# Linear attention with gated experts: a written order of all units found anew, and the place where a flag is read

## The chip, the cores and the metric

The kernel runs on one core of a Trainium2 chip. The time is device time in microseconds (us). It is the median of 3 runs. PE is TensorE, DVE is VectorE, ACT is ScalarE, POOL is GpSimd, and SP is the engine that issues most transfers here.

## The reference

Two stages follow each other. The first is linear attention, the second sends each token through one of eight experts:

```python
q_p, k_p = (phi(q), phi(k))          # phi(x) = (x if x > 0 else exp(x) - 1) + 1
kv = np.einsum('bhsd,bhse->bhde', k_p, v)
z = np.sum(k_p, axis=2)
num = np.einsum('bhsd,bhde->bhse', q_p, kv)
den = np.einsum('bhsd,bhd->bhs', q_p, z)[..., None] + 1e-06
x = num / den                        # (8, 8, 576, 64) -> x: (8, 576, 512)
...
logits = x @ w_gate                  # 8 experts
local_gate = sigmoid(x @ w_local)
for b in range(B):
    for s in range(S):
        fresh_e = argmax(logits[b, s])
        e = fresh_e if s == 0 or local_gate[b, s] < 0.5 else prev_e
        h = np.maximum(x[b, s] @ w1[e], 0.0)
        out[b, s] = softmax(logits[b, s])[e] * (h @ w2[e])
```

Batch 8, heads 8, sequence 576, head dimension 64; w1 is 8 x 512 x 1024, w2 is 8 x 1024 x 512.

## The kernel before

The kernel takes for granted that all tokens of a batch use the expert of its first token, and counts the tokens for which that would be wrong. Only if the count (the flag) is over zero does it run a general path behind the main one, which these inputs don't reach.

The main path is cut into units, each of which is one function. A string, ORDER, names all units in the order in which they are written into the program. Each engine takes its own instructions strictly in that order, and semaphores hold it back where data or a buffer is not ready. A number behind a slash names one of four PSUM slots of two banks; the next unit in a slot waits until the last one there has been read out. A batch is a (0 to 7), and half a batch's heads is n = 2a + j (0 to 15). The units:

- Lk.n, Lv.n, Lq.n: SP issues the load of k, v or q (576 KB). There are 4 buffers for k, 3 for v and 2 for q, so Lk.6 waits until K.2 has read its buffer, Lq.7 until P.q.5 is done. Lwg loads the gate's weights. SP also issues the stores ST and, in HOLD, a tiny copy that waits for the first expert's weights.
- E.x.n, E2.x.n: exp and relu on ACT (x is k or q); P.x.n: DVE combines them to phi; CL.n, P0.0 and E0.0 are forms of this for the first batch. VC.n copies v beside a column of ones (DVE; VC.0 on ACT).
- K.n: PE's 36 small matmuls of k with v (tile kvps, 64x64 tiles, line 297), KC.n copies the result out (DVE).
- Q.n, QL.a: transposes of q on PE (tq, tql), QC.n and QLC.a copy them out (ACT).
- N.a.j.h, NL.a: q with kv (nps, npl, 64x64 tiles, line 349 and 368); D and DL divide on DVE.
- X.a.h, XL.a: transposes of the quotient (tx, txl); XC, XLC copy them to xT (DVE).
- R.a.0, R.a.1: the gate's logits (lps; R.a.0 has 64 columns of the array); RC copies them out; PK.a picks the expert, BK.a books it in a small table of which weights are on the core; W.a.0 and W.a.1 have POOL load w1 and w2 if they are missing; CW.a.x copies them to the place of use (DVE). S1, S2, S3 work out the probability.
- H.a.m: the hidden layer in 8 pieces of 8 matmuls (hps, line 532), HC.a.m applies the relu (ACT). O0.a and O.a.0 to O.a.4: the output layer (yps, lines 551 and 555; O.a.4 uses 128x64); OC.a.i scales and evicts (ACT).
- FL, TOT, FI count the flag (DVE, PE, DVE); FR.e has engine e read it into a register, ahead of its branch at the end.

The first matmuls, on a tile of zeros (fill, line 705), only keep PE busy until data comes.

Of the kernel before, what the change touches and what calls it, by code (L numbers as in the profile page):

```python
# [24 lines left out]
P.k.1 K.0/2 Lwg E2.q.0 VC.1 P.q.0.0 K.1/3 Lv.3 P.q.0 E.q.1 KC.0 KC.1 Lk.2 E2.q.1 NL.0/1 Q.0/2 Lq.2 DL.0
E.k.3 P.q.1.0 WG QC.0 XL.0/3 XLC.0 P.q.1 R.0.0/1 E2.k.3 N.0.0.1/3 RC.0.0 Lq.3 PK.0 Q.1/2 Lv.2 D.0.0.1 W.0.0
N.0.0.0/1 QC.1 VC.3 E.q.2 D.0.0.0 N.0.1.1/3 N.0.1.0/2 BK.0 D.0.1.1 E.k.2 W.0.1 D.0.1.0 E.q.3 X.0.1/1 P.k.3
E2.k.2 X.0.0/3 E2.q.3 XC.0.0 K.3/2 XC.0.1 E2.q.2 R.0.1/0 H.0.0/3 P.q.2 H.0.1/1 HC.0.0 RC.0.1 P.q.3 H.0.2/3
HC.0.1 H.0.3/0 HOLD P.k.2 HC.0.2 Lq.4 QL.1/1 H.0.4/3 Lq.5 QLC.1 KC.3 VC.2 HC.0.3 Lk.5 Q.3/2 Lk.4 CW.0.0
HC.0.4 Q.2/1 S1.0 H.0.5/0 QC.2 H.0.6/3 S2.0 HC.0.5 QC.3 K.2/1 HC.0.6 N.1.1.1/0 KC.2 Lv.6 N.1.0.1/2 D.1.1.1  # L30
E.q.4 NL.1/3 H.0.7/1 D.1.0.1 O0.0/0 HC.0.7 DL.1 E2.q.4 S3.0 O.0.0 XL.1/2 E.q.5 X.1.1/1 XLC.1 P.q.4 O.0.1/3
OC.0.0 E.k.5 XC.1.1 Lq.6 R.1.0/2 Lv.5 N.1.0.0/0 RC.1.0 OC.0.1 Lv.4 PK.1 N.1.1.0/1 E.k.4 O.0.2/2 D.1.1.0
W.1.0 E2.q.5 D.1.0.0 O.0.3/3 E2.k.5 P.q.5 OC.0.2 X.1.0/1 OC.0.3 O.0.4/0 XC.1.0 Lq.7 E.q.6 Lk.7 CW.1.0
R.1.1/2 QL.2/3 Q.4/1 QLC.2 RC.1.1 E2.k.4 CW.0.1 H.1.0/3 OC.0.4 VC.5 Q.5/2 W.1.1 HC.1.0 VC.4 QC.4 H.1.1/0
P.k.4 Lv.7 E.q.7 Lk.6 H.1.2/3 BK.1 H.1.3/1 HC.1.1 P.k.5 HC.1.2 K.4/0 E2.q.6 S1.1 K.5/3 HC.1.3 KC.4 CW.1.1
S2.1 QC.5 H.1.4/0 Lk.9 P.q.6 H.1.5/1 HC.1.4 KC.5 Lq.8 VC.6 N.2.0.1/2 HC.1.5 ST.0.0 NL.2/0 E.k.6 D.2.0.1
N.2.0.0/3 N.2.1.0/1 Lk.8 E.k.7 DL.2 Lv.8 H.1.6/2 ST.0.4 D.2.1.0 H.1.7/0 HC.1.6 S3.1 E2.k.7 XL.2/1 O0.1/2
D.2.0.0 HC.1.7 O.1.0 XLC.2 O.1.1/0 VC.7 OC.1.0 P.k.7 E2.k.6 R.2.0/3 E2.q.7 N.2.1.1/1 P.k.6 K.7/2 E.q.8
RC.2.0 P.q.7 O.1.2/3 E.k.9 KC.7 Lq.9 D.2.1.1 OC.1.1 X.2.0/2 E.k.8 K.6/0 XC.2.0 PK.2 OC.1.2 QL.3/1 Lk.10
X.2.1/2 QLC.3 Lv.9 Q.7/3 E2.k.8 KC.6 W.2.0 XC.2.1 Lk.11 Q.6/1 QC.7 P.k.8 NL.3/0 QC.6 O.1.3/2 DL.3 W.2.1  # L40
E2.q.8 VC.8 R.2.1/3 BK.2 E.q.9 XL.3/1 O.1.4/0 XLC.3 RC.2.1 CW.2.0 R.3.0/1 K.8/3 OC.1.4 E.k.10 VC.9 H.2.0/0
Lk.12 RC.3.0 KC.8 Lv.10 S1.2 H.2.1/1 HC.2.0 PK.3 OC.1.3 N.3.1.1/3 HC.2.1 P.q.8 N.3.1.0/0 W.3.0 E2.q.9
H.2.2/2 D.3.1.0 E2.k.9 Lq.10 H.2.3/1 D.3.1.1 HC.2.2 H.2.4/0 HC.2.3 P.k.9 H.2.5/2 HC.2.4 N.3.0.1/3 P.q.9
HC.2.5 K.9/1 E.q.10 D.3.0.1 Lq.11 N.3.0.0/0 E2.k.10 H.2.6/2 D.3.0.0 Q.9/3 HC.2.6 CW.2.1 S2.2 QL.4/0 Q.8/2
QLC.4 S3.2 W.3.1 QC.9 H.2.7/0 KC.9 VC.10 X.3.1/1 HC.2.7 P.k.10 O0.2/3 E2.q.10 XC.3.1 QC.8 X.3.0/0 P.q.10
O.2.0 NL.4/1 E.k.11 O.2.1/2 XC.3.0 Lq.12 OC.2.0 DL.4 E2.k.11 R.3.1/0 CW.3.0 XL.4/3 O.2.2/1 E.k.12 RC.3.1
XLC.4 E.q.11 O.2.3/0 OC.2.1 OC.2.2 N.4.1.1/3 OC.2.3 N.4.0.0/2 O.2.4/1 D.4.0.0 K.10/0 OC.2.4 D.4.1.1 E2.q.11
R.4.0/2 N.4.0.1/1 Lk.14 KC.10 Lv.11 H.3.0/3 P.q.11 Lv.12 ST.1.0 H.3.1/0 HC.3.0 D.4.0.1 H.3.2/3 ST.2.4 HC.3.1
RC.4.0 BK.3 H.3.3/1 Lv.13 HC.3.2 P.k.11 ST.1.4 QL.5/2 HC.3.3 H.3.4/0 CW.3.1 QLC.5 H.3.5/3 HC.3.4 Lk.13 S1.3
E.q.12 Q.11/1 VC.11 PK.4 HC.3.5 X.4.1/2 H.3.6/0 QC.11 Lq.13 W.4.0 K.11/3 HC.3.6 E2.q.12 N.4.1.0/1 KC.11  # L50
XC.4.1 N.5.1.1/0 E2.k.12 D.4.1.0 W.4.1 NL.5/3 H.3.7/2 S2.3 E.k.14 D.5.1.1 O0.3/1 HC.3.7 S3.3 X.4.0/0 DL.5
O.3.0 Q.10/2 P.k.12 OC.3.0 XL.5/3 O.3.1/1 XLC.5 E.k.13 XC.4.0 P.q.12 QC.10 R.4.1/3 O.3.2/0 CW.4.0 OC.3.1
Lq.14 Lv.14 E.q.13 O.3.3/2 VC.12 RC.4.1 N.5.0.1/1 OC.3.3 K.12/3 OC.3.2 D.5.0.1 O.3.4/2 KC.12 N.5.0.0/0
OC.3.4 R.5.0/1 E2.q.13 N.5.1.0/3 ST.3.4 RC.5.0 D.5.0.0 X.5.1/2 H.4.0/1 Lk.15 D.5.1.0 ST.2.0 H.4.1/0 HC.4.0
BK.4 E.q.14 Lv.15 H.4.2/3 PK.5 HC.4.1 H.4.3/1 P.q.13 HC.4.2 W.5.0 H.4.4/0 E2.k.13 XC.5.1 H.4.5/3 Lq.15
HC.4.3 S1.4 HC.4.4 QL.6/2 VC.13 Q.12/1 S2.4 HC.4.5 P.k.13 H.4.6/0 QLC.6 CW.4.1 H.4.7/3 HC.4.6 QC.12 X.5.0/2
W.5.1 K.13/0 HC.4.7 E2.k.14 N.6.0.0/1 KC.13 XC.5.0 N.6.0.1/3 E.k.15 NL.6/0 D.6.0.1 O0.4/2 E2.k.15 S3.4 O.4.0
E2.q.14 O.4.1/3 D.6.0.0 E.q.15 DL.6 O.4.2/1 E2.q.15 OC.4.0 P.q.15 Q.13/0 OC.4.1 O.4.3/2 QC.13 VC.15 CW.5.0
# [12 lines left out]
"""


# [1 line left out]
def kernel(  # L75
# [44 lines left out]
    with ExitStack() as main:  # L120
# [481 lines left out]
        def load_flag(engine):  # L602

            for r in flag_r:
                if r.engine == engine:
                    nc.reg_load(r, flag_i[0:1, 0:1])
# [345 lines left out]
```

## Time and profile before

| what | value |
|---|---|
| median of 3 runs | 223.32 us (222.03 to 223.62) |
| profiled execution | 224.62 us, of which span 222.4 us |
| PE, ACT, DVE, POOL busy | 206.8, 153.2, 151.6, 12.3 us |
| granted clock of PE | 0.996 |
| moved by DMA | 46.77 MB |

The span goes from the first to the last instruction of the program; 2.2 us of the profiled time lie around it. The profiled execution is one run, and 1.3 us above the median. PEld is PE's weight load, which overlaps its matmuls. A wait is put down to what ended it last; "issue" is time in which an engine waited for nothing that the profile shows.

### The profile page before, as it was taken

Reading aid. Unit: us, or ns where it says so; the run is one execution under the profiler, and the core shown is the slowest. Engines: PE = TensorE matmul, PEld = TensorE weight load, DVE = VectorE, ACT = ScalarE, POOL = GpSimd, SP = SyncE. Lnnn points to the kernel's source line nnn. Section 1 sums busy time; section 2 is a strip of 40 time slices with the busy share of each in tenths; the row PEclk is TensorE's granted clock in tenths of the full one; section 3 lists DMA queues with packets and bytes.
Section 4 is the critical chain, followed back from the end, with each engine's and each line's share of the span. In section 5 each row is a group of like instructions: output and inputs, shape, how many; then the busy total and the mean of one; then the engine's idle time right before and its main releaser. Section 6 shows DMA issues by size and latency. Waiting matters only on the chain.

```text
span 222.4 us, 8532 instructions
## 1 busy us (share of the span) xinstructions
PE 206.8 (93%) x3695; PEld 149.7 (67%) x3711; DVE 151.6 (68%) x428; ACT 153.2 (69%) x226; POOL 12.3 (6%) x41
## 2 busy tenths in 40 slices
...
GB/s 194 385 347 330 218 208 392 126 247 272 233 178 401 174 316 215 208 227 222 67 266 406 198 212 101 376 221 204 113 309 4 3 93 134 186 183 2 27 322 90
DMA packets 24141, 46.77 MB, mean 210 GB/s; under 512 B 2834, under 2 KB 8978, under 8 KB 23202
## 3 DMA queue, kind: packets, MB, share of 16 engines
...
q8 instruction: 31, 0.51, 0.9%
q10 hardware_dynamic: 432, 0.20, 0.4%
q14 instruction: 12, 0.10, 0.1%
...
## 4 chain that ended last, share of the span: by engine, by line
PE 84%; DMA 6%; DVE 3%; issue 2%; ACT 2%; SPq 0%; DVEq 0%; ACTq 0%
PE hps L532 27%; PE yps L551 25%; PE nps L349 8%; PE kvps L297 7%; PE tq L308 6%; PE tx L383 3%; PE yps L555 3%; DMA qraw<-in_q_dram 3%; DMA kraw<-in_k_dram 3%; PE lps L416 1%; DVE kraw L271 1%; PE npl L368 1%; PE lps L410 1%; PE fill L705 1%; PE tql L322 1%
## 5 line engine op out<-in xcount | busy, mean ns | idle before, releaser
L532 PE MATMUL hps<-xT,w1cur 128*128 128x288 bf16 x512 | 66.9, 286 | 0.8 <-issue 0.8
L551 PE MATMUL yps<-w2cur,hT 128*128 128x512 bf16 x241 | 58.4, 379 | 0.8
L532 PEld LDWEIGHTS <-w1cur 128*128 128x128 bf16 x512 | 48.7, 98 | 13.7 <-issue 1.3
L539 ACT ACTIVATE hT<-hps 128x576 bf16<-128x576 f32 x64 | 41.2, 652 | 24.3 <-PE hps L532 24.2
L551 PEld LDWEIGHTS <-hT 128*128 128x128 bf16 x256 | 24.1, 98 | 25.5 <-issue 0.2
L565 ACT ACTIVATE yo<-yps,pr 128x512 f32<-128x512 f32 x32 | 21.3, 686 | 12.9 <-PE yps L551 10.1
L276 DVE SCALAR_TENSOR_TENSOR fq<-fq,qraw 128x576 f32<-128x576 f32 (+1 forms) x32 | 22.5, 740 | 2.8 <-ACT qraw L247 2.8
L297 PE MATMUL kvps<-vone,kraw 64*64 64x65 f32 x1152 | 19.9, 220 | 3.2 <-ACT hT L539 1.2
L337 DVE TENSOR_TENSOR xb<-nps,rec 128x512 bf16<-128x512 f32 x32 | 22.1, 691 | 1.1
L349 PE MATMUL nps<-kv,qT 64*64 64x65 f32 x1024 | 21.1, 222 | 1.1 <-ACT qT L314 0.6
L297 PEld LDWEIGHTS kvps<-vone,kraw 64*64 64x64 f32 x1152 | 18.2, 134 | 5.4 <-ACT hT L539 1.5
L314 ACT COPY qT<-tq 128x512 f32<-128x512 f32 x32 | 18.3, 640 | 4.5 <-PE tq L308 4.5
L349 PEld LDWEIGHTS nps<-kv,qT 64*64 64x64 f32 x1024 | 17.6, 134 | 4.9 <-issue 2.7
L241 ACT ACTIVATE ek<-kraw 128x1152 f32<-128x1152 f32 x16 | 18.5, 1162 | 2.6 <-DMA kraw<-in_k_dram 2.2
L241 ACT ACTIVATE fq<-qraw 128x1152 f32<-128x1152 f32 (+1 forms) x16 | 18.5, 1156 | 2.4 <-DMA qraw<-in_q_dram 2.2
L269 DVE SCALAR_TENSOR_TENSOR kraw<-ek,kraw 128x1152 f32<-128x1152 f32 x14 | 18.8, 1346 | 0.3 <-ACT kraw L247 0.3
L247 ACT ACTIVATE qraw<-qraw 128x1152 f32<-128x1152 f32 (+1 forms) x16 | 18.3, 1150 | 0.1
L308 PE MATMUL tq<-ident,fq 128*128 128x128 f32 x128 | 16.4, 274 | 0.0
L247 ACT ACTIVATE kraw<-kraw 128x1152 f32<-128x1152 f32 x14 | 16.4, 1168 | 0.0
L308 PEld LDWEIGHTS tq<-ident,fq 128*128 128x128 f32 x128 | 14.3, 141 | 0.5
L388 DVE COPY xT<-tx 128x1024 bf16<-128x1024 bf16 x16 | 10.8, 681 | 3.5 <-PE tx L383 3.5
L302 DVE COPY kv<-kvps 128x130 f32<-128x130 f32 x16 | 4.6, 289 | 11.3 <-PE kvps L297 11.2
...
## 6 DMA issues: line engine op xcount, KB each, us to landing
...
```

The lines of the kernel that those rows point to most:

```text
L241: nc.scalar.activation(e[:, :, c0:c1, :], raw_, Act.Exp)
L247: nc.scalar.activation(raw_, raw_, Act.Relu)
L269: nc.vector.scalar_tensor_tensor(r, e, 1.0, r, Alu.min, Alu.add)
L276: nc.vector.scalar_tensor_tensor(e[:, g], e[:, g], 1.0, r[:, g], Alu.min, Alu.add)
L297: nc.tensor.matmul(ps[g * PH:(g + 1) * PH, t, :W], lhsT=f[h, g, c, :], rhs=vo[h, g, c, :], start=(c == 0), stop=(c == C - 1))
L308: nc.tensor.transpose(ps[:, r, i * P:(i + 1) * P], ex_[n, "q"][:, 1 + i + (NC - 1) * r, :, :], identity=ident)
L337: nc.vector.tensor_tensor(dst, ps[:, :, :, :Dh].rearrange("p g (i t) e -> p g i t e", t=2), rec.rearrange("p g (i t o) -> p g i t o", t=2, ...
L349: nc.tensor.matmul(ps[o * PH:(o + 1) * PH, g, (il * 2 + t) * W:(il * 2 + t + 1) * W], lhsT=qT[n][g * PH:(g + 1) * PH, t, i * P + o * PH:i ...
L532: nc.tensor.matmul(ps[:, u, :HS], lhsT=w1b[:, kk, m * P:(m + 1) * P], rhs=xT[b][:, kk, u * HS:(u + 1) * HS], start=(kk == 0), stop=(kk == ...
L539: nc.scalar.activation(hT[b][:, m, :].rearrange("p (u s) -> p u s", u=2), open_.pop(("H", b, m))[:, :, :HS], Act.Relu)
L551: nc.tensor.matmul(ps, lhsT=hT[b][:, m, i * P:(i + 1) * P], rhs=w2b[:, m, :], start=(m == 0), stop=(m == FK - 1))
L565: nc.scalar.activation(ym[:, i, :], ps, Act.Copy, scale=pr[:, i:i + 1])
```

## The change

The whole of ORDER is replaced: the same units stand in another order, and many have another PSUM slot. The lengths of units from which the order is found now count changes of the array's tiling. The number of instructions that compute is the same. The places at which the flag is read are given by ORDER alone, as before; a table beside it, which the program did not use, goes:

```diff
 ORDER = """
-Lk.1 FILL/0 Lk.0 Lv.0 Lq.0 Lv.1 E.k.1 Lq.1 E0.0 CL.0 E.k.0 CL.1 Lk.3 P0.0 VC.0 P.k.0 QL.0/1 QLC.0 E.q.0
...
+Lk.1 FILL/0 Lv.0 Lk.0 Lq.0 Lv.1 Lq.1 Lwg E.k.1 CL.1 Lk.3 E0.0 P.k.1 VC.0 P0.0 Lv.3 E.k.0 CL.0 QL.0/1 Lk.2
...
-        after = {"DVE": ("FI",), "POOL": ("FI",), "SP": ("ST", B - 1, 2), "ACT": ("OC", B - 1, 2),
-                 "PE": ("O", B - 1, NC - 1)}
-        for e, d in after.items():
+        for e in ENG:
             op(("FR", e), lambda e=e: load_flag(ENG[e]))
```

Three places of the new order. In the opening, v0 is loaded ahead of k0 and the gate's weights ahead of k3. PE first runs N.0.0.0, N.0.0.1, Q.1, N.0.1.0, N.0.1.1 and K.3, then X.0.1 and X.0.0; it had K.3 behind the X units. Behind the first hidden units, at about 38 us, ACT before was written as

```order
L539 ACTIVATE hT<-hps 128x576
L241 ACTIVATE fq<-qraw_72 128x2x9x64
L539 ACTIVATE hT<-hps 128x576
L247 ACTIVATE qraw_72<-qraw_72 128x1152
L241 ACTIVATE fq<-qraw_73 128x2x9x64
L565 ACTIVATE yo<-yps,pr 128x512
```

(HC.0.6, E.q.4, HC.0.7, E2.q.4, E.q.5, OC.0.0), and is now

```order
L539 ACTIVATE hT<-hps 128x576 x3
L241 ACTIVATE ek<-kraw_69 128x1152
L241 ACTIVATE ek<-kraw_70 128x1152
L565 ACTIVATE yo<-yps,pr 128x512
L247 ACTIVATE kraw_69<-kraw_69 128x1152
```

(HC.0.5 to HC.0.7, E.k.5, E.k.6, OC.0.0, E2.k.5): k is worked on ahead of q. At the end, SP reads the flag behind its last store instead of ahead of its last two, ACT reads it behind HC.7.3 instead of behind OC.7.2, and TOT stands between H.7.2 and H.7.3 instead of between O0.7 and O.7.0.

More of the change, by code (lines that the diff above doesn't have):

```diff
@@ L23 @@
 ORDER = """
-Lk.1 FILL/0 Lk.0 Lv.0 Lq.0 Lv.1 E.k.1 Lq.1 E0.0 CL.0 E.k.0 CL.1 Lk.3 P0.0 VC.0 P.k.0 QL.0/1 QLC.0 E.q.0
[L25 to L58, printed above, removed]
@@ L69 @@
-HC.7.6 O0.7/3 HC.7.7 OC.6.1 TOT/2 O.7.0 ST.6.0 FI O.7.1/0 OC.7.0 FR.DVE FR.POOL ST.6.4 O.7.2/1 OC.7.1 ST.7.0
-O.7.3/2 OC.7.2 FR.ACT ST.7.2 O.7.4/3 OC.7.3 FR.SP FR.PE OC.7.4 ST.7.3 ST.7.4
+Lk.1 FILL/0 Lv.0 Lk.0 Lq.0 Lv.1 Lq.1 Lwg E.k.1 CL.1 Lk.3 E0.0 P.k.1 VC.0 P0.0 Lv.3 E.k.0 CL.0 QL.0/1 Lk.2
+QLC.0 P.k.0 E.q.0 E2.q.0 K.0/2 VC.1 P.q.0.0 K.1/3 KC.0 E.q.1 P.q.0 KC.1 Lq.2 NL.0/1 E2.q.1 Q.0/2 DL.0 WG
+P.q.1.0 QC.0 XL.0/3 E.k.3 XLC.0 P.q.1 R.0.0/1 N.0.0.0/2 RC.0.0 Lq.3 PK.0 N.0.0.1/3 E2.k.3 Lv.2 Q.1/1 D.0.0.0
@@ new lines @@
+N.1.0.1/3 RC.1.0 OC.0.0 PK.1 N.1.1.1/0 E2.k.5 O.0.1/1 XC.1.0 W.1.0 E.q.4 D.1.0.1 O.0.2/2 E.q.5 D.1.1.1
+OC.0.1 P.k.5 X.1.1/3 E2.q.4 O.0.3/0 VC.5 OC.0.2 CW.1.0 E2.q.5 K.5/1 E2.k.6 XC.1.1 O.0.4/2 P.q.5 OC.0.3
+H.1.0/3 OC.0.4 E.k.4 P.q.4 R.1.1/0 H.1.1/2 HC.1.0 KC.5 Lq.6 CW.0.1 QL.2/1 Lq.7 HC.1.1 H.1.2/3 E2.k.4 RC.1.1
+VC.4 W.1.1 H.1.3/2 Lv.7 HC.1.2 P.k.4 Q.5/0 QLC.2 HC.1.3 H.1.4/3 S1.1 QC.5 P.k.6 K.4/1 S2.1 E.q.6 N.2.1.1/2
+KC.4 Lk.8 HC.1.4 CW.1.1 NL.2/0 Lv.8 E2.q.6 Q.4/1 DL.2 H.1.5/3 E.q.7 D.2.1.1 H.1.6/0 HC.1.5 P.q.6 XL.2/2
@@ new lines @@
+VC.9 H.2.1/1 OC.1.4 D.3.0.0 Lv.12 HC.2.0 ST.0.4 H.2.2/0 P.q.8 HC.2.1 H.2.3/2 HC.2.2 R.3.0/3 HC.2.3 H.2.4/1
+RC.3.0 P.q.9 E2.k.10 H.2.5/0 HC.2.4 PK.3 Lq.11 QL.4/3 E2.k.9 Lq.10 Q.9/2 VC.10 W.3.0 H.2.6/1 HC.2.5 P.k.9
+H.2.7/0 HC.2.6 P.k.10 QLC.4 R.2.1/1 HC.2.7 N.3.1.0/3 QC.9 N.3.1.1/0 RC.2.1 CW.2.1 K.9/1 E.k.12 S1.2 W.3.1
+Q.8/2 KC.9 S2.2 D.3.1.0 E.q.10 O0.2/1 D.3.1.1 QC.8 NL.4/3 E2.k.12 N.4.1.1/0 DL.4 K.10/2 VC.11 S3.2 O.2.0
+O.2.1/3 KC.10 OC.2.0 E.k.11 X.3.1/2 O.2.2/1 D.4.1.1 OC.2.1 E.q.11 XC.3.1 XL.4/3 X.3.0/0 BK.3 OC.2.2 O.2.3/2
```

44 lines of the change are left out of this document (34 added, 10 removed).

## The prediction

> **What bounds the kernel now.** I read the page first, then the windows, the chain of waits, the waits by engine and last the timeline. The page says which engine is full:
>
> ```profile
> span 222.4 us, 8532 instructions
> PE 206.8 (93%) x3695; PEld 149.7 (67%) x3711; DVE 151.6 (68%) x428; ACT 153.2 (69%) x226; POOL 12.3 (6%) x41
> PE 84%; DMA 6%; DVE 3%; issue 2%; ACT 2%; SPq 0%; DVEq 0%; ACTq 0%
> ```
>
> PE is busy for 206.8 of 222.4 us and makes 84% of the chain that ended last. The windows (columns: length, then busy time of PE, PEld, DVE, ACT, POOL, granted clock, DMA share, GB/s) tell where its 15.6 idle us lie:
>
> ```profile
> 0.00:14.00 14.00, 9.78 (x167) 5.10 (x169) 7.12 (x14) 8.74 (x12) 2.29 (x17) 1.00 0.88 301
> 20.00:26.00 6.00, 3.60 (x155) 2.95 (x149) 5.65 (x13) 5.83 (x7) 2.38 (x3) 1.00 1.15 291
> 40.00:60.00 20.00, 18.71 (x287) 13.28 (x289) 17.44 (x49) 16.90 (x23) 0.57 (x3) 1.00 0.64 219
> 100.00:120.00 20.00, 19.95 (x391) 14.80 (x394) 14.02 (x41) 15.60 (x24) 0.22 (x2) 1.00 0.81 222
> 217.00:222.40 5.40, 0.00 (x0) 0.00 (x0) 0.00 (x0) 0.40 (x1) 0.00 (x0) 0.85 0.28 85
> ```
>
> The opening loses 4.2 us to 14 and 2.4 between 20 and 26, the stretch 40 to 60 loses 1.3, and the end 5.4. From 60 to 217 next to nothing is idle (0.05 us of 100 to 120). So a new order can win in three ways: fewer us inside PE's busy time, fewer waits between 26 and 60, or a shorter end. DVE is busy 17.4 of 20 us between 40 and 60 and ACT 16.9, so they have little to give there.
>
> **Switches of tiling.** This is the part of the busy time that an order can change. K, N and NL run the array as four 64x64 tiles; R.a.0 and O.a.4 use 128x64; the rest is 128x128. The chain of waits lists the same unit with and without a switch ahead of it (start, us, engine and line, matmuls):
>
> ```profile
> 32.13 0.98 PE hps L532 x8
> 93.57 1.09 PE hps L532 x8
> 119.07 1.21 PE kvps L297 x72
> 92.05 1.05 PE kvps L297 x72
> 134.22 0.63 PE nps L349 x32
> 93.10 0.47 PE nps L349 x32
> ```
>
> One hidden unit takes 0.98 us behind another 128x128 unit, 1.09 behind 64x64 work. One K takes 1.05 behind an N, 1.21 behind hidden work; one N 0.47 behind K, 0.63 behind O.a.4. So entering 64x64 costs 0.16 us, leaving it 0.11; the mean is 0.135.
>
> I counted the changes of tiling along PE's written order: 73 before, 61 now. Ahead of the first hidden unit it is 11 and 9, where PE waits anyway; behind it 62 and 52. That is 10 switches less where PE is full. The place around K.6 shows how. On PE before, between the transposes of batch 2 (tx, tql are 128x128; kvps is K.6):
>
> ```order
> L383 LDWEIGHTS xb_1290
> L383 MATMUL tx<-identb,xb_1290 128x128
> L297 MATMUL kvps<-vone_77,kraw_70 64x65 x36
> L322 MATMUL tql<-ident,fq 128x128 x2
> L383 LDWEIGHTS xb_1229
> ```
>
> and now, behind the gate's short logits R.2.0 (64x9):
>
> ```order
> L410 LDWEIGHTS xT
> L410 MATMUL lps<-wg,xT 64x9
> L349 MATMUL nps<-kv,qT 64x65 x32
> L297 MATMUL kvps<-vone_77,kraw_70 64x65 x36
> L549 LDWEIGHTS hT
> ```
>
> K.6 stood alone and paid two switches; it now stands behind two N units and shares theirs. **Term 1:** 10 x 0.135 = 1.4 us less; 12 x 0.16 = 1.9 if those of the opening count too, 10 x 0.11 = 1.1 at the low end. I take 1.5, since one or two in the opening fall where PE is not waiting.
>
> **The opening.** The loads go out as k1, v0, k0 instead of k1, k0, v0, and Lwg ahead of k3. DVE's four divisions of batch 0, v3's copy, P.k.3 and the two copies to xT must all end ahead of R.0.1, in either order, and DVE is full there (5.65 of 6 us). H.0.0 also needs the first expert's weights, which follow from DVE's PK.0, at the same place behind the same work. **Term 2:** 0 us, between -0.4 and +0.4.
>
> **The waits between 26 and 60.** The waits on PE:
>
> ```profile
> PE kvps L297 <- ACT hT L539: 1.2, 1, 1.2
> PE tx L383 <- issue: 0.9, 1, 0.9
> PE hps L532 <- issue: 0.8, 1, 0.8
> PE nps L349 <- issue: 0.3, 1, 0.3
> ```
>
> The first is a load that comes late, by the chain:
>
> ```profile
> 50.30 6.68 DMA qraw<-in_q_dram
> 57.09 1.16 ACT fq L241
> 58.25 0.55 ACT hT L539
> 58.84 2.33 PE kvps L297 x144
> ```
>
> q7 was issued at 50.30 and landed 6.68 us later; E.q.7 stands on ACT ahead of HC.1.1, and K.4 needs the PSUM slot that HC.1.1 empties. In the new order E.q.7 stands ahead of HC.1.5, and HC.1.1 has no load ahead of it that late. **Term 3:** this wait of 1.2 us goes.
>
> In its place comes another. On SP before, from the wait for the first weights on (kraw_69, 68 are k5, k4; qraw_72, 73 are q4, q5):
>
> ```order
> L486 DMA there<-w1cur 1x1
> L138 DMA qraw_72<-in_q_dram 128x2x576
> L138 DMA qraw_73<-in_q_dram 128x2x576
> L138 DMA kraw_69<-in_k_dram 128x2x576
> L138 DMA kraw_68<-in_k_dram 128x2x576
> ```
>
> and now:
>
> ```order
> L486 DMA there<-w1cur 1x1
> L138 DMA kraw_69<-in_k_dram 128x2x576
> L138 DMA kraw_70<-in_k_dram 128x2x576
> L138 DMA qraw_72<-in_q_dram 128x2x576
> L138 DMA qraw_73<-in_q_dram 128x2x576
> L138 DMA vraw_76<-in_v_dram 128x2x576
> L138 DMA kraw_68<-in_k_dram 128x2x576
> ```
>
> The second load is now k6, into the buffer that K.2 reads, and six more loads queue on SP behind it. Their rows, with the evictions on ACT that follow:
>
> ```profile
> 30.39 0.89 SPq L138 DMA_DIRECT2D qraw<-in_q_dram  x2
> 36.81 1.21 PE kvps L297 x72
> DMA to landing us min/median/max: 3.6/5.8/9.2
> L539 ACT ACTIVATE hT<-hps 128x576 bf16<-128x576 f32 x64 | 41.2, 652 | 24.3 <-PE hps L532 24.2
> L565 ACT ACTIVATE yo<-yps,pr 128x512 f32<-128x512 f32 x32 | 21.3, 686 | 12.9 <-PE yps L551 10.1 <-DVE pr L525 2.7
> ```
>
> K.2 ends at 38.0 (36.81 + 1.21) in both, since the same units stand ahead of it. So q4, issued at 30.4 before, goes out only behind k6 at 38.0. On ACT the new order has HC.0.7, E.k.5, E.k.6, OC.0.0, where it had HC.0.7, E2.q.4, E.q.5, OC.0.0. PE after K.2 runs two N and NL.1 (1.3), waits 0.5 for instructions (below), then H.0.7 (1.0), O0.0 and O.0.0 (1.7), and by now X.1.0, R.1.0 and two N (2.0): it wants O.0.1, in the slot that OC.0.0 empties, at 44.5. ACT has H.0.7 at 40.8, HC.0.7 done at 41.5, E.k.5 at 42.6, then E.k.6 (1.16) and OC.0.0 (0.69) at 44.5. No slack is left: each us that k6 takes beyond 4.6 is one us of PE. The landings of kraw (third row) are 3.6 to 9.2 us, median 5.8; the queue is empty by 38, which speaks for the low end. **Term 4:** +0.5, between 0 and 4.6 (9.2 - 4.6). E.q.6 and E.q.7 then stand ahead of HC.1.4 and HC.1.5, again with loads that went out late: +0.3, 0 to 0.8.
>
> **Instructions.** The three waits on "issue" lie 256 PE instructions apart: between two of them the windows count 128 + 127 and 126 + 126, and an own queue brings blocks of 0.51 MB / 31 = 16 KB:
>
> ```profile
> 23.09:30.99 7.90, 6.21 (x128) 4.87 (x127) 6.68 (x10) 6.28 (x7) 0.00 (x0) 1.00 1.23 203
> 30.99:38.41 7.42, 7.13 (x126) 6.10 (x126) 3.39 (x8) 5.15 (x12) 0.18 (x1) 1.00 1.10 337
> q8 instruction: 31, 0.51, 0.9%
> ```
>
> PE ran out of instructions while the DMA engines were full (share 1.23 and 1.10), and each block took 7.9 and 7.4 us. The two at 31 and 38 lie among the same units in the new order and stay. But grouping 64x64 units makes blocks denser: R.2.0, two N and K.6 are 16 + 128 + 144 instructions in 0.2 + 1.0 + 1.2 = 2.4 us; with O0.1 ahead a block there lasts about 4 us. The densest of the old order between 40 and 60 is K.4 and K.5, 288 instructions in 2.33 us, without a wait at its block's end. **Term 5:** +0.3, 0 to 3.5 (7.4 - 4).
>
> [...]
>
> **The end.** SP's read of the flag stood between the last two stores and is now behind them; ACT's moves from behind OC.7.2 to behind HC.7.3:
>
> ```profile
> L606 ACTq TENSOR_LOAD <-flag_i x1: 492/492/492, 214.2 to 214.2; - x1
> L606 SPq TENSOR_LOAD <-flag_i x1: 962/962/962, 216.1 to 216.1; - x1
> 215.93 0.69 ACT L565 ACTIVATE yo<-yps,pr 128x512 f32<-128x512 f32 x1 [1.04 <-PE yps L551]
> 217.43 1.56 ACTq L579 DMA_DIRECT2D out_dram<-yl  x2
> ```
>
> SP's read ran from 216.1 to 217.1, while OC.7.3 was done at 216.6; the store waited 0.45 us. But what ends the run is ACT's last store (217.43 to 218.99), behind O.7.4 and OC.7.4, which SP's earlier store helps only by leaving the queue sooner; the read itself then runs while that store lands. ACT's read waits for the flag, which PE's TOT now makes three hidden units sooner. **Term 6:** -0.2, between -0.45 and 0.
>
> **Small waits.** PE's other idle time behind 26 is some 1 us before. The new order leaves less room between a unit and the next in its slot (OC.1.1, QC.7 and QC.10 each stand behind one or two loads' work), so I add **term 7:** +0.4, -0.5 to +1.2.
>
> **Sum.** -1.5 + 0 - 1.2 + 0.8 + 0.3 - 0.2 + 0.4 = -1.4 us. Against the profiled execution, span 222.4 and time 224.62, that is 221.0 and 223.2. The three timed runs have their median at 223.32, 1.3 below the profiled one, so I forecast 223.32 - 1.4 = **221.9 us**. One per cent, 2.2 us, is about what a measurement of this kernel can tell from no change (its runs lie 222.03 to 223.62).
>
> **Rivals.** A, all of it pays: the loads land in 4 us, no block is late, the small waits halve. Then -1.9 - 1.2 - 0.45 - 0.5 = -4.1 at the best, -3.0 in the middle: 220.3. For it: the queue is idle when k6 goes out. Against: no slack at O.0.1.
>
> B, slower: k6 is late. SP holds seven loads behind K.2; they then land one after the other, and k6 shares the DMA engines with instruction blocks. At 9.2 us PE waits 4.6 us for OC.0.0's slot in place of 0.5, and the sum is -1.4 + 4.1 = +2.7: 226.0. From a landing of 6.5 us on (4.6 + 0.5 + 1.4) the change no longer gains. For it: before, loads issued at 30.4 landed late behind the weights. Against: those weights are in by 38.
>
> C, starved of instructions: the dense block at K.6 takes as long as those at 31 and 38, 3.2 us more than in the sum, +1.8: 225.1. Against: DMA's share is 0.64 between 40 and 60, half of what it was there.
>
> D, the change doesn't do what it says: a switch costs nothing where PE waits for ACT next anyway, so term 1 turns into waits on ACT and DVE, which are busiest from 40 to 60: -1.4 + 1.5 = +0.1, 223.4.
>
> **How the numbers follow.** Forecast 0.48, A 0.22, B 0.12, C 0.06, D 0.12. The forecast's own range is 220.6 to 223.3; a third of its chance lies below 221.1, the 1% line: 0.16. Faster: 0.16 + 0.20 of A = 0.36. Slower (over 225.55): 0.10 of B, 0.02 of C = 0.12, and 0.52 for the same. The range takes A's middle and most of B: 219.6 to 225.6.
>
> **What would show it.** Right: PE's busy time falls by 1.3 to 2 us with the same count of matmuls; kvps no longer waits 1.2 us on ACT; the waits on "issue" near 31 and 38 stay. Wrong: PE waits over 1 us at yps for ACT's yo near 44.5 (B), "issue" near 67 to 69 (C), or PE's busy time falls and its idle time rises by as much (D).

## The result, and the profile after

The changed kernel takes **229.76 us** (median of 4 runs, 229.03 to 230.99), the kernel before beside it 223.19 (4 runs): ratio 1.031, interval 1.025 to 1.037. It is 6.6 us slower, where 1.4 us less was forecast, and lies 4.2 us above the range. Medians here and below are over all runs of a kernel, since the runs of these orders scatter by 1 to 3%; the ratios with an interval leave out runs over 1.5% above the fastest.

The page of the profiled execution (229.03 us, span 227.4):

```profile
span 227.4 us, 8556 instructions
PE 206.8 (91%) x3711; PEld 150.4 (66%) x3711; DVE 152.2 (67%) x428; ACT 153.5 (68%) x226; POOL 14.7 (6%) x41
PEclk9979999999999999999999999999999999999998
```

PE's busy time is what it was, 206.8, although there are fewer changes of tiling. The 7 in the third slice of the clock's row, a stretch at half clock (0.50 from 11.07 to 14.48), explains only a part of that: from H.0.0 to O.7.4 the clock is full in both profiles, and PE is busy for 185.7 us before and 185.6 now. (The profile before lacks 15 records of yps, x241 for x256, and its row of them is 0.7 us shorter; some of the saving may be hidden there.) So the 5.0 us of span are idle time. The windows (columns as before) show where:

```profile
0.00:14.00 14.00, 8.98 (x115) 4.99 (x119) 6.85 (x12) 8.21 (x11) 2.29 (x17) 0.90 0.88 292
40.00:60.00 20.00, 19.83 (x358) 14.18 (x359) 17.88 (x45) 18.64 (x26) 0.67 (x3) 1.00 0.88 315
80.00:100.00 20.00, 18.35 (x427) 14.91 (x418) 17.49 (x53) 17.28 (x25) 1.65 (x2) 1.00 0.93 264
100.00:120.00 20.00, 18.74 (x302) 13.68 (x302) 14.80 (x35) 11.87 (x16) 0.18 (x1) 1.00 0.63 150
120.00:140.00 20.00, 18.59 (x428) 13.33 (x429) 14.86 (x54) 15.99 (x24) 1.38 (x4) 1.00 0.82 278
140.00:160.00 20.00, 16.99 (x288) 12.85 (x287) 11.98 (x32) 13.52 (x22) 1.47 (x2) 1.00 0.75 160
```

40 to 60 gained 1.1 us, about the wait of term 3 (19.83 busy for 18.71). But 80 to 160, where PE had next to no idle time, now loses 7.3 us. The waits on PE name what for:

```profile
PE nps L349 <- issue: 2.7, 1, 2.7
PE kvps L297 <- ACT hT L539: 2.6, 1, 2.6
...
PE kvps L297 <- ACT qT L328: 1.4, 1, 1.4
PE nps L349 <- ACT qT L314: 1.2, 1, 1.2
PE kvps L297 <- DVE kraw L271: 1.2, 1, 1.2
```

The 1.2 us of kvps for ACT's hT at 57 is gone, and so are the waits on "issue" at 31 and 38. Three new ones are long, one each. The first, at 98 us, in the timeline (start, length, engine and line, in brackets the idle time before it and what ended that):

```profile
92.60 0.77 POOL L480 DMA_DIRECT2D w1s<-in_moe_w_dram  x1 [15.98 <-DVE kraw L269]
95.59 0.88 POOL L480 DMA_DIRECT2D w2s<-in_moe_w_dram  x1 [2.22 <-DVE t L507]
98.10 0.41 PE L349 MATMUL nps<-kv,qT 64*64 64x65 f32 x15
101.25 0.50 PE L349 MATMUL nps<-kv,qT 64*64 64x65 f32 x17 [2.75 <-issue]
```

N.4.1.1 stops after 15 of its 32 matmuls, for no semaphore: a block of instructions ends there (the kernel before had 255 and 252 of PE's from one such wait to the next). It is made of K.9, Q.8, O0.2, NL.4 and half of N.4.1.1 and ran for only some 4.4 us, while POOL's loads of the third expert's weights filled the DMA engines (share 1.01 from 92.60 to 98.30).

The second, at 119, and the third, at 149:

```profile
113.28 0.37 SPq L138 DMA_DIRECT2D qraw<-in_q_dram  x1
119.75 1.16 ACT L241 ACTIVATE fq<-qraw 128x1152 f32<-128x1152 f32 x1 [1.90 <-DMA qraw<-in_q_dram]
120.95 0.41 ACT L328 COPY qT<-tql 128x128 f32<-128x128 f32 x2
121.41 1.28 PE L297 MATMUL kvps<-vone,kraw 64*64 64x65 f32 x72 [1.42 <-ACT qT L328]
...
138.91 0.48 SPq L138 DMA_DIRECT2D qraw<-in_q_dram  x1
149.98 1.16 ACT L241 ACTIVATE fq<-qraw 128x1152 f32<-128x1152 f32 x1 [3.37 <-DMA qraw<-in_q_dram]
151.05 0.63 ACT L539 ACTIVATE hT<-hps 128x576 bf16<-128x576 f32 x1
151.74 1.28 PE L297 MATMUL kvps<-vone,kraw 64*64 64x65 f32 x72 [2.59 <-ACT hT L539]
```

q12 lands 6.4 us after its issue and q15 11.0. ACT stands at E.q.12 and E.q.15 until then, 1.9 and 3.4 us. Behind E.q.12 is QLC.5, which empties the slot that K.11 wants; behind E.q.15 is HC.4.6, whose slot K.13 wants. This is the very chain of q7, HC.1.1 and K.4 that the change took away, twice.

The opening is the fourth place. K.0 and K.1 before, and then now:

```profile
10.73 1.28 PE L297 MATMUL kvps<-vone,kraw 64*64 64x65 f32 x72 [0.38 <-ACT qT L328]
12.63 1.28 PE L297 MATMUL kvps<-vone,kraw 64*64 64x65 f32 x72 [0.61 <-DVE vone L288]
```

```profile
11.51 3.68 PE L297 MATMUL kvps<-vone,kraw 64*64 64x65 f32 x144 [1.20 <-DVE kraw L271]
```

Together they took 3.68 us, at half clock from 11.07 to 14.48; each took 1.28 before. H.0.0 starts at 27.93 and not at 26.89.

| stretch (PE's starts) | before | after | difference |
|---|---|---|---|
| to H.0.0 | 26.89 | 27.93 | +1.04 |
| H.0.0 to H.1.0 | 25.81 | 24.43 | -1.38 |
| H.1.0 to H.2.0 | 31.47 | 31.03 | -0.44 |
| H.2.0 to H.3.0 | 26.33 | 28.08 | +1.75 |
| H.3.0 to H.4.0 | 25.59 | 26.39 | +0.80 |
| H.4.0 to H.5.0 | 21.99 | 25.78 | +3.79 |
| H.5.0 to O.7.4 | 57.74 | 57.74 | 0.00 |
| O.7.4 to the end | 6.58 | 6.02 | -0.56 |

Summed another way, an estimate from the starts of PE's units, each set against its length without a change of tiling: the changes cost 9.2 us before and 7.3 after (-1.8), waits and half clock 9.0 and 16.5 (+7.4), the end -0.6. That is the 5.0 us of span. The other timed runs of the change have a mean clock of 0.971 to 0.975 instead of 0.990, and spans 0.6 to 2.0 us longer; by an estimate two or three more stretches at half clock would fit that (one of 3.41 us takes 0.0075 off the mean), but those runs have no trace.

### The profile page after: what moved, and what is told of

The parts are those of the page before. It is cut to its first block, busy times and chain, and to the rows that moved or that the text cites. A ratio compares the mean times of both kernels' runs of the same rounds, so it can differ in the third digit from the quotient of the medians.

```text
span 227.4 us, 8556 instructions
## 1 busy us (share of the span) xinstructions
PE 206.8 (91%) x3711; PEld 150.4 (66%) x3711; DVE 152.2 (67%) x428; ACT 153.5 (68%) x226; POOL 14.7 (6%) x41
## 5 line engine op out<-in xcount | busy, mean ns | idle before, releaser
L551 PE MATMUL yps<-w2cur,hT 128*128 128x512 bf16 x256 | 59.1, 379 | 0.5 <-ACT qT L314 0.3
L551 PEld LDWEIGHTS <-hT 128*128 128x128 bf16 x256 | 24.2, 98 | 25.9 <-issue 0.4
L297 PE MATMUL kvps<-vone,kraw 64*64 64x65 f32 x1152 | 21.5, 228 | 5.9 <-ACT hT L539 2.6
L297 PEld LDWEIGHTS kvps<-vone,kraw 64*64 64x64 f32 x1152 | 19.7, 143 | 8.2 <-ACT hT L539 2.8
L349 PE MATMUL nps<-kv,qT 64*64 64x65 f32 x1024 | 20.2, 221 | 4.4 <-issue 2.7
L269 DVE SCALAR_TENSOR_TENSOR kraw<-ek,kraw 128x1152 f32<-128x1152 f32 x14 | 18.7, 1348 | 1.8 <-ACT kraw L247 1.8
L494 DVE COPY w1cur<-w1s 128x4096 bf16 x7 | 8.6, 1223 | 7.2 <-DMA w1s<-in_moe_w_dram 6.4
```

The lines of the kernel that those rows point to most:

```text
L269: nc.vector.scalar_tensor_tensor(r, e, 1.0, r, Alu.min, Alu.add)
L297: nc.tensor.matmul(ps[g * PH:(g + 1) * PH, t, :W], lhsT=f[h, g, c, :], rhs=vo[h, g, c, :], start=(c == 0), stop=(c == C - 1))
L349: nc.tensor.matmul(ps[o * PH:(o + 1) * PH, g, (il * 2 + t) * W:(il * 2 + t + 1) * W], lhsT=qT[n][g * PH:(g + 1) * PH, t, i * P + o * PH:i ...
L551: nc.tensor.matmul(ps, lhsT=hT[b][:, m, i * P:(i + 1) * P], rhs=w2b[:, m, :], start=(m == 0), stop=(m == FK - 1))
```

## The experiments

Difference is the median less that of the kernel before, which ran beside each. Where a kernel has four runs, a difference of 1 us can be chance.

| run | median | before | difference | ratio (interval) |
|---|---|---|---|---|
| the change | 229.76 | 223.19 | +6.6 | 1.031 (1.025 to 1.037) |
| two exponentials moved on ACT | 225.82 | 223.85 | +2.0 | 0.997 (0.992 to 1.002) |
| O units first | 229.22 | 223.85 | +5.4 | 1.022 (1.015 to 1.029) |
| more fills | 233.84 | 223.85 | +10.0 | 1.044 (1.039 to 1.049) |
| k0 first | 229.65 | 223.85 | +5.8 | 1.020 (1.015 to 1.026) |
| no third weights | 227.38 | 223.54 | +3.8 | 1.020 (1.014 to 1.026) |
| dummy 64x64, on before | 231.50 | 223.54 | +8.0 | 1.038 (1.033 to 1.043) |
| dummy 128x128, on before | 225.08 | 223.54 | +1.5 | 1.010 (1.004 to 1.016) |
| three moves | 223.47 | 223.54 | -0.1 | 0.998 (0.995 to 1.002) |
| opening of before | 228.81 | 223.75 | +5.1 | 1.021 (1.015 to 1.027) |
| opening and moves | 223.19 | 223.75 | -0.6 | 0.998 (0.995 to 1.001) |
| flag read last, on before | 223.33 | 223.75 | -0.4 | 0.999 (0.995 to 1.004) |
| two more moves | 223.36 | 223.43 | -0.1 | 1.001 (0.998 to 1.005) |

**Two exponentials moved on ACT.**

```diff
-H.3.5/2 HC.3.4 E.q.12 H.3.6/3 ... QLC.5 HC.3.5 K.11/0 QC.10 ... HC.3.6
+H.3.5/2 HC.3.4 H.3.6/3 ... QLC.5 HC.3.5 K.11/0 QC.10 ... HC.3.6 E.q.12
-HC.4.5 E.q.15 Q.13/3 H.4.7/1 HC.4.6 E2.k.15 X.5.0/2 K.13/0 HC.4.7 QC.13
+HC.4.5 Q.13/3 H.4.7/1 HC.4.6 E2.k.15 X.5.0/2 K.13/0 HC.4.7 QC.13 E.q.15
```

> The changed kernel with two exponentials moved on ACT and nothing else: E.q.12 from ahead of QLC.5 to behind HC.3.6, E.q.15 from ahead of HC.4.6 to behind QC.13. Theory (loads that land late stand on ACT ahead of evictions that PE needs): the waits of 1.5 us at K.11 and 2.7 us at K.13 go, with 0.5 behind the latter, and the time falls by 4.2 to 4.7 us, to 225.1 to 225.6. Rival (PE's idle time comes from the two loads themselves, whose consumers follow soon anyway): the waits move to Q.12 and Q.15 or to the N units of batch 6 and at least half of them stays, 227.5 or more. Rival (the rest of the schedule is bound by ACT): below 1 us is gained.

Measured: 225.82, 4.6 us less against the kernel beside it (10 runs, 221.6 to 227.98). The ratio of 0.997 rests on the four shortest of them; by these the gain would be larger still. The trace, of a run of 225.85, agrees with the 4.6: from H.3.0 to H.5.0 it has 47.54 us, the change 52.17. Windows of this kernel:

```profile
120.00:140.00 20.00, 19.74 (x439) 14.26 (x438) 16.00 (x59) 16.13 (x24) 1.38 (x4) 1.00 0.88 310
140.00:160.00 20.00, 20.00 (x311) 14.51 (x311) 15.12 (x39) 14.87 (x24) 2.37 (x2) 1.00 0.80 164
```

PE is full again where it had 18.59 and 16.99. Neither rival holds: nothing comes back at Q.12 or Q.15, so the loads were never late for their own consumers, only for what stood behind them. Two words of the order are two thirds of the loss.

**O units first.** The block of instructions at 98 us is made longer.

```diff
-O0.2/1 ... NL.4/3 ... N.4.1.1/0 ... K.10/2 ... O.2.0 O.2.1/3 ... X.3.1/2 O.2.2/1 ... XL.4/3 X.3.0/0
+O0.2/1 ... O.2.0 O.2.1/3 ... X.3.1/0 O.2.2/1 ... NL.4/3 ... N.4.1.1/0 ... K.10/2 ... XL.4/3 X.3.0/0
```

> The changed kernel with one stretch of PE's order around 98 us turned: O.2.0, O.2.1, X.3.1 and O.2.2 go ahead of NL.4, N.4.1.1 and K.10 (their evictions, copies and the gate's S3.2 go along on ACT and DVE, slots are given anew). The number of instructions is the same; the block of 256 that ran for 4.3 us there now lasts about 9 us. Theory (the next block of instructions takes 7 us to come while the third expert's weights are loaded, and a block that runs for less waits for it): the wait of 2.97 us goes and the time falls by 2.5 to 3.0 us, to 226.8 to 227.3. Rival (the wait belongs to the place in time, whatever the block holds): it stays at 2 to 3 us at the next boundary, and the time stays within 1 us of 229.8. Rival (the N and K units behind it now come too late): a wait of over 1 us for DVE's copies at XL.4 or R.4.0 takes its place, 228 or more.

Measured: 229.22, only 1.2 us less. The wait of 2.75 us is gone, and from H.2.0 to H.3.0 the trace has 26.48 us for 28.08; but its opening, where PE ran at half clock from 24.2 to 27.6, took 1.5 us more than in the change's trace. And another wait came (timeline of this kernel):

```profile
106.76 0.69 DVE L335 TENSOR_TENSOR xb<-nps,rec 128x512 bf16<-128x512 f32 x1
...
107.51 0.62 PE L381 MATMUL tx<-identb,xb 128*128 128x128 bf16 x8 [1.24 <-DVE xb L335]
```

It is X.3.0, whose slot D.4.1.1 has to empty, and D.4.1.1 now stands late on DVE behind VC.11 and KC.10. So the third case of the expectation holds, one unit further on than named there.

**More fills.**

```diff
-    fills = {("QL", 0): 19, ("K", 0): 2, ...
+    fills = {("QL", 0): 27, ("K", 0): 6, ...
```

> The changed kernel with 27 instead of 19 warming matmuls ahead of QL.0 and 6 instead of 2 ahead of K.0, nothing else; 12 matmuls of 0.21 us at full clock, 2.6 us, for some 3.4 us of PE's idle time there. Theory (the clock fell to half from 11.07 to 14.48 us because PE stood idle from 7.1 to 9.5 and 10.3 to 11.5): the granted clock stays at 1.0 from its rise on, K.0 and K.1 take 2.6 us together and not 3.7, H.0.0 starts 0.8 to 1.1 us sooner than 27.93, and the runs' mean clocks rise to 0.985 and more: 228.0 to 229.0. Rival (what starts late in the opening is set by the loads and DVE, which the clock doesn't touch): H.0.0 moves by less than 0.3 us. Rival (the fall is a matter of when the run starts within the clock's own period): the clock falls as before in some run.

Measured: 233.84, the worst of all, and my theory of the opening fell. The clock did stay up through K.0 and K.1 (2.33 us for both). But the 12 matmuls bring 24 instructions, so the two blocks of the opening end 12 matmuls sooner than with the two exponentials: behind 7 matmuls of R.0.0 and not behind 11 of N.0.0.0, and behind 54 of N.0.1.0 and N.0.1.1 and not behind 2 of K.3 (timeline, and the row of the clock):

```profile
18.92 0.17 PE L410 MATMUL lps<-wg,xT 128*64 128x9 bf16 x1 [0.94 <-issue]
25.36 0.59 PE L349 MATMUL nps<-kv,qT 64*64 64x65 f32 x10 [1.86 <-issue]
```

```profile
PEclk9999559999999999999999999999999999999996
```

PE waited 0.94 and 1.86 us for instructions, in R.0.0 and in N.0.1.1, and then ran from 24.4 to 34.7 at half clock. H.0.0 started at 30.96. In the 3.41 us ahead of the fall PE had stood still for 2.1, 1.2 of them for QC.1 and 0.9 for instructions. So more matmuls don't hold the clock here: they bring waits for instructions.

**k0 first.**

```diff
-Lk.1 FILL/0 Lv.0 Lk.0 Lq.0 Lv.1 Lq.1 Lwg E.k.1 CL.1 Lk.3 E0.0 P.k.1 VC.0 P0.0 Lv.3 E.k.0 CL.0 QL.0/1 Lk.2 QLC.0 P.k.0 E.q.0
+Lk.1 FILL/0 Lk.0 Lv.0 Lq.0 Lv.1 Lq.1 Lwg E.k.1 E0.0 CL.0 E.k.0 CL.1 Lk.3 P0.0 VC.0 Lv.3 P.k.0 QL.0/1 Lk.2 QLC.0 P.k.1 E.q.0
```

> The changed kernel with its first 22 steps put as in the kernel before: k0 loaded ahead of v0, E0.0, CL.0 and E.k.0 ahead of CL.1, P0.0 and VC.0, and P.k.1 behind P.k.0; all behind it as in the change. Theory (half of the 1.04 us that the opening lost by H.0.0 is k0, which lands behind v0): K.0 starts at 10.7 and not 11.5 us, H.0.0 0.4 to 1.0 us sooner, 228.8 to 229.4. Rival (only the clock's fall cost time): K.0 starts sooner but H.0.0 moves by less than 0.2 us, unless the clock too stays up. Rival (DVE's work up to R.0.1 sets H.0.0): no change.

Measured: 229.65, 0.8 us less (four runs, 227.5 to 231.45, so that by the times alone it could be chance), and H.0.0 at 27.20, 0.7 us sooner, as the theory had it, but not for its reason. K.0 did start at 10.59, but R.0.0 starts at 17.08 here and at 17.14 in the kernel with the two exponentials, whose K.0 started at 11.49. So k0's delay was made up by then. What differs is the wait in K.3 (this kernel, then the other):

```profile
23.57 1.27 PE L295 MATMUL kvps<-vone,kraw 64*64 64x65 f32 x70 [0.15 <-issue]
```

```profile
25.16 1.27 PE L295 MATMUL kvps<-vone,kraw 64*64 64x65 f32 x70 [1.39 <-issue]
```

PE's order is the same in both; its instructions came 0.15 us late in one execution and 1.39 in the other, and with a like wait in N.0.0.0 (0.42 and 0.86) H.0.0 is at 27.20 and 28.79.

**No third weights.**

```diff
-                    in_=src, cond=wl[b][2] > 0)
+                    in_=src, cond=wl[b][2] > (1 if b == 3 else 0))
-                wd[b] = reg(rt[b][2][0:1, 0:1], ET.DVE, NS - 1)
+                wd[b] = reg((first if b in (3, 4) else rt[b][2])[0:1, 0:1], ET.DVE, NS - 1)
```

> The changed kernel without the transfer of the expert that batch 3 misses (two loads of 1 MB in the DRAM's float32, 92.6 to 107.5 us); batches 3 and 4 use the expert of slot 0 instead, so their outputs are another expert's. The order and every instruction on PE stay. Theory (the block of instructions that PE needs at 98.3 us comes late because these loads fill the DMA engines): the wait of 2 to 3 us at N.4.1.1 goes or falls below 0.5, and with it the fall of the clock behind it, -2.5 to -3.5 us: 226.3 to 227.3. Rival (a block of 256 instructions that runs for 4.3 us is too short whatever else is loaded): the wait stays above 2 us. Rival (PE waits there for something other than instructions, which the profile doesn't name): it stays unchanged too, but the block's own packets come before 98 us.

Measured: 227.38, 2.7 us less. Windows of the change, and then of this kernel, over the same stretch:

```profile
92.60:98.30 5.70, 5.70 (x200) 4.55 (x198) 4.99 (x13) 5.70 (x11) 1.65 (x2) 1.00 1.01 222
98.30:101.20 2.90, 0.21 (x15) 0.07 (x6) 2.14 (x9) 0.61 (x1) 0.00 (x0) 1.00 1.14 201
```

```profile
92.60:98.30 5.70, 5.65 (x182) 4.51 (x184) 5.29 (x14) 5.70 (x12) 0.26 (x2) 1.00 0.35 132
98.30:101.20 2.90, 2.74 (x125) 2.24 (x123) 2.41 (x11) 1.11 (x2) 0.00 (x0) 1.00 0.02 6
```

With the DMA engines' share at 0.35 and 0.02 in place of 1.01 and 1.14, PE runs from one block of 256 into the next after 4.4 us without a pause. The block itself, 16 KB in the queue of instructions (q8), moves between 98.7 and 100 us in the change, when PE has stopped already, and between 94 and 96.6 us here; so the rival of a wait for something else falls. A block of 4.4 us does no harm by itself, and beside the loads a longer block, of some 8 us by the count, did not wait (O units first): here it takes both.

**Two dummies.** What a change of tiling costs, apart from any order.

```diff
                 for kk in range(DK): ...
+                if u == 0 and m in (2, 3, 4, 5):
+                    nc.tensor.matmul(ps[:PH, 0, 500:501], lhsT=w1b[:PH, 0, :PH],
+                                     rhs=w1b[:PH, 0, :1], start=True, stop=True)
```

The second has P (128) in place of PH (64).

> The kernel before with one matmul of 64x64 by one column put into hidden units 2 to 5 of every batch, between their two halves (32 in all, written to a column that nothing reads). Each adds a change of tiling into 64x64 and one back: 64 changes. Theory (a change costs 0.135 us on the mean, 0.16 in and 0.11 out): each of these units is 0.27 us longer plus the matmul itself, 32 x 0.3 = 9 us: 232 to 233. Rival (a change costs nothing of its own, the 73 to 61 saves nothing): under 0.1 us each, 223 to 227, the same as with a matmul of 128x128 in that place.

> The kernel before with one matmul of 128x128 by one column in the same 32 places: as many instructions, no change of tiling. Both theories: 0.03 to 0.1 us each, 1 to 3 us, 224.5 to 227; the difference to the one of 64x64 is the price of 64 changes.

Measured: 231.50 and 225.08. Timelines of the first and the second, from one dummy to the next, a hidden unit's worth of matmuls:

```profile
88.44 0.19 PE L536 MATMUL hps<-w1cur 64*64 64x1 bf16 x1
...
89.64 0.19 PE L536 MATMUL hps<-w1cur 64*64 64x1 bf16 x1
```

```profile
87.61 0.17 PE L536 MATMUL hps<-w1cur 128*128 128x1 bf16 x1
...
88.62 0.17 PE L536 MATMUL hps<-w1cur 128*128 128x1 bf16 x1
```

1.20 us for 1.01: a change in and one back cost 0.19, and over the whole kernel (231.50 - 225.08) / 64 = 0.10 us each. So a change has a price of its own, somewhat below my 0.135 (the dummies are bf16 matmuls of one column, my rows fp32 ones of 65), and the time stayed just below the theory's range.

**Three moves.** k0 first, the two exponentials, and the O units again, this time with NL.4 left ahead of them.

```diff
-O0.2/1 ... NL.4/3 ... N.4.1.1/0 ... K.10/2 ... O.2.0 O.2.1/3 ... X.3.1/2 O.2.2/1 ... XL.4/3
+O0.2/1 ... NL.4/3 ... O.2.0 O.2.1/0 ... X.3.1/2 O.2.2/1 ... N.4.1.1/0 ... K.10/2 ... XL.4/3
```

> The changed kernel with three stretches of its order turned: the opening's loads as before (k0 ahead of v0), E.q.12 and E.q.15 behind the evictions on ACT, and O.2.0, O.2.1, X.3.1 and O.2.2 ahead of N.4.1.1 and K.10 (NL.4 stays ahead of them this time, so that its divisions are done when XL.4 comes). Theory (the waits are apart from each other and add): -0.6 - 4.6 - 2.7, so 221.5 to 222.5, 1 to 2 us below the kernel before. Rival (instructions are what PE lacks, and a wait taken away at one block's end is given back at the next, as the wait of 1.4 us at XL.4 did when NL.4 was moved): 224 or more.

Measured: 223.47, the time of the kernel before (ratio 0.998, 0.995 to 1.002): 6.6 us are back, but not the 1 to 2 us below it. Timeline:

```profile
25.07 1.28 PE L295 MATMUL kvps<-vone,kraw 64*64 64x65 f32 x70 [1.40 <-issue]
...
107.61 1.24 PE L549 MATMUL yps<-w2cur,hT 128*128 128x512 bf16 x5 [0.94 <-issue]
```

The opening still waits, and at 107 so does the end of the block that took N.4.1.1 and K.10 over. Neither range is met: of the 2.75 us at N.4.1.1 0.94 move on, and the rest is a gain, so theory and rival each hold in part, in shares of about 2 to 1.

**The opening of before,** alone and with the moves.

```diff
-Lk.1 FILL/0 Lv.0 Lk.0 ... N.0.0.0/2 ... N.0.0.1/3 ... Q.1/1 ... N.0.1.0/2 N.0.1.1/1 ... K.3/3 ... X.0.1/1 ... X.0.0/2 ... R.0.1/1 H.0.0/2
+Lk.1 FILL/0 Lk.0 Lv.0 ... N.0.0.1/3 ... Q.1/2 ... N.0.0.0/1 ... N.0.1.1/3 N.0.1.0/2 ... X.0.1/1 ... X.0.0/2 ... K.3/3 ... R.0.1/1 H.0.0/2
```

> The changed kernel with everything ahead of H.0.0 in the order of the kernel before, on all engines; from H.0.0 on the order of the change. As many PE instructions stand ahead of H.0.0, so the blocks of 256 end at the same later units. Theory (the new order of the opening costs 1.0 to 2.5 us by itself: K.3 ahead of the transposes of x, N.0.1.0 right behind Q.1, so that waits for instructions and for QC.1 both push the transposes): H.0.0 at 26.9 instead of 27.9 to 28.8, the time 1 to 2 us less, 227.5 to 228.5. Rival (the opening is bound by DVE and the loads, and what the runs show there is chance): H.0.0 between 27.5 and 29 again.

> The same opening, and the two moves behind it: E.q.12 and E.q.15 behind the evictions, the O units of batch 2 ahead of N.4.1.1 and K.10. Theory (waits add): 1 to 1.9 us below the kernel with the three moves and the new opening (223.47), so 221.6 to 222.5, and below the kernel before by the 1.8 us of the switches less what K.8 and O.2.3 still wait for instructions (1.1 and 0.9 us): 222 to 222.9. Rival (the wait for instructions moves on to later blocks): 223.4 or more.

Measured: alone 228.81, 1.5 us less, H.0.0 at 27.49 (its K.3 ran at half clock); with the moves 223.19 (ratio 0.998, 0.995 to 1.001), 0.5 less than with the new opening. Timeline of the latter:

```profile
22.99 0.49 PE L381 MATMUL tx<-identb,xb 128*128 128x128 bf16 x6 [0.87 <-issue]
...
26.81 5.07 PE L530 MATMUL hps<-xT,w1cur 128*128 128x288 bf16 x40
```

A block ends here too, and PE waits 0.87 us for the next. But N.0.0.0 stands between Q.1 and the N units that need QC.1, and X.0.1 begins at 21.84 instead of 25.27 as in the change, so H.0.0 is at 26.81. In the seven traces with the opening of before H.0.0 starts at 26.81 to 27.79, in the six with the new one (more fills left out, k0 first in two) at 27.20 to 29.39, on the mean 1.1 us later; the times give 1.5 and 0.5. So the new opening costs about 1 us by its order. The time with the moves lies between theory and rival.

**Flag read last.**

```diff
-OC.7.3 FR.SP FR.PE OC.7.4 ST.7.3 ST.7.4
+OC.7.3 FR.PE OC.7.4 ST.7.3 ST.7.4 FR.SP
```

> The kernel before with SP's read of the flag behind the last two stores, as the change has it, and nothing else (ACT's read and the sum over the flags stay). Theory (SP's 0.96 us of reading delayed a store that then ended ahead of ACT's last one): the store goes out 0.45 us sooner, the end of the run moves by 0 to 0.45 us: the stretch from O.7.4 to the end 6.1 to 6.6 us. Rival (what shortened that stretch by 0.56 us in the change is ACT's read, which stood behind the last but one eviction): it stays at 6.5 or more.

Measured: 223.33 (ratio 0.999, 0.995 to 1.004). The stores of the output (count, durations, first and last start): before, this kernel, the change:

```profile
L574 SPq DMA_DIRECT2D out_dram<-yo x20: 472/588/1299, 63.4 to 217.7; - x20
```

```profile
L572 SPq DMA_DIRECT2D out_dram<-yo x20: 471/591/1183, 62.3 to 216.0; - x20
```

```profile
L574 SPq DMA_DIRECT2D out_dram<-yo x20: 471/592/1847, 82.1 to 222.7; - x20
```

The last one goes out 1.9, 1.3 and 1.3 us behind the start of O.7.4 (215.82, 214.71, 221.38). So the move brings that store forward by 0.6 us, and the end by 0.1 (6.58 to 6.49). But the rival isn't shown by that: the kernels with the dummies read the flag as the kernel before does, and end 6.1 and 6.0 us behind O.7.4 (223.00 and 216.58, spans 229.1 and 222.6). So 0.56 us is no more than what executions with one and the same end differ by, and neither read is shown to be worth anything. In all five traces ACT issues its last stores 1.6 us behind O.7.4.

**Two more moves,** on the opening and the moves.

```diff
-Q.6/0 ... Q.7/2 ... K.7/3
+Q.6/0 ... K.7/2 ... Q.7/3
-K.10/2 ... XL.4/3 X.3.0/0 ... O.2.3/2
+O.2.3/2 ... K.10/3 ... XL.4/2 X.3.0/0
```

> The kernel with the opening of before and the moves at 98, 119 and 149 us (223.19), with two more stretches of PE's order turned, each to make a dense block of instructions last longer: K.7 between Q.6 and Q.7 instead of behind both, so that the block that ends in K.8 at 80 us takes 0.75 us more; and O.2.3 ahead of K.10 instead of behind XL.4 and X.3.0, so that the block that ends at 105.5 us takes 0.9 us more. Theory (a block that ends before the next has come waits for just the difference): the waits of 0.73 us at K.8 and 1.1 us at O.2.3 go down to 0.3 and less each, with no new one of that size: 1.2 to 1.6 us less, 221.6 to 222.2, and below the kernel before by 0.5 to 1%. Rival (the wait moves to the next block's end): the sum of the waits on instructions behind 40 us stays at 1.6 us or more, 222.8 to 223.8.

Measured: 223.36 (ratio 1.001, 0.998 to 1.005). Both waits for instructions are gone and nothing is gained. In their place stands, among the waits on PE,

```profile
PE lps L408 <- DVE xT L386: 1.3, 1, 1.3
```

R.4.0, for a copy on DVE that now comes later; and each of the two turns adds two changes of tiling, 4 x 0.10 = 0.4 us by the dummies' price. No version was found that is surely faster than the kernel before.

## Why the prediction was wrong, step by step

- **Term 1** (switches, -1.5): right in size, -1.8 by the units' lengths and 12 x 0.10 = 1.2 by the dummies' price. But the sign that was named for it did not come: PE's busy time did not fall by 1.3 to 2 us. Of rival D the free switch falls; that a part of the saving turns into other waits holds (last paragraph).
- **Term 2** (opening, 0 +- 0.4): failed. +1.0 in the profile, +0.3 to +1.9 in three others with this opening and full clock (k0 first in two), 1.1 on the mean of all. The step "the same work on DVE ahead of R.0.1, in either order" left out PE: QC.1 is now waited for (1.2 us for 0.6), K.3 stands ahead of the transposes, and the waits for instructions fall into units that these need.
- **Term 3** (the wait for q7 goes, -1.2): right.
- **Term 4** (k6, +0.8): right in place. k6 was issued at 38.19 and landed 4.4 us later, O.0.1 started at 44.44, with a wait of 0.2 for the +0.8. That it fits the 44.5 worked out is in part luck: 0.5 of that was a wait for instructions that did not come. Rival B falls.
- **Term 5** (instructions, +0.3, 0 to 3.5): right mechanism, wrong places. "The two waits at 31 and 38 stay" was wrong. The blocks still end among the same units (as many PE instructions stand ahead of H.0.0 in both orders, H.0.0 to H.0.3 follow, and K.2 again has as many ahead of it), but the instructions came in time. From 35 to 39 us the DMA engines' share is 0.28, for 1.04 before, since the loads now stand behind k6 and so behind K.2, which is term 4's own reason; why the wait at 31 went, at a share of 1.19 for 1.23, isn't shown. And the dense block that I priced, at K.6, passed; the one at N.4.1.1 cost 2.75 us and a smaller one at K.8 0.2. Rival C had named the cause, at the wrong unit. I had judged by DMA's share of 40 to 60, and not looked for the blocks that end while an expert's weights are loaded; the order and the loads of before show both.
- **Term 6** (end, -0.2): -0.56, just outside, but ends of the same order differ by as much (6.0 to 6.6 us), so nothing of it is shown to come from the reads.
- **Term 7** (small waits, +0.4, up to 1.2): the term that decided. It measured 4.6 us, in two waits of the kind of term 3. I had followed the loads' slack at one place, O.0.1, and put all other loads into a lump sized by what was idle before. QC.7, OC.1.1 and QC.10, which I named, cost 0.3 at the most.

The sum failed since a new order was priced by the waits that it removes, each looked up in the trace, and by the waits that it adds at one place. The rest of the program had next to no idle time before, and the prediction took it that the new order would keep it so; it was in fact a balance of that order alone.

With the three stretches put back as they were or turned, about half of the change's own gain is eaten up by what is left: against the kernel before, the profile of the kernel with the opening and the moves has 1.3 us less in changes of tiling and 0.7 more in waits. The medians differ by 0.6 us, which the interval doesn't tell from nothing.
